# Last block of a routed expert kernel: early products and W2 splits written out in program order, and the next expert's rows asked for ahead of its weights

## The chip, the cores and the metric

The kernel runs on one core of one Trainium2 chip. The metric is device time in microseconds (us) of one launch. TensorE does the matrix products, VectorE and ScalarE the elementwise work and the evictions from PSUM, GpSimd (POOL) some elementwise work and the indirect DMAs, SyncE (SP) issues the other DMAs.

## What is computed

Three parts run one after the other. A linear attention with decay (2 batches, 8 heads, 768 positions, head size 64, blocks of 64 positions) gives x of 1536 tokens by 512. A gated layer follows, and then a layer of eight experts of which each token uses two:

```
x = sigmoid(x @ w_gate) * (x @ w_val) @ w_out            # 512 -> 1536 -> 512

noisy = x @ w_gate2 + log1p(exp(x @ w_noise)) * noise    # 8 logits a token
top2  = two largest of noisy;  top2_w = softmax over the two
for e in range(8):
    h = max(x[tokens of e] @ w1[e], 0)                   # 512 -> 1024
    out[tokens of e] += top2_w * (h @ w2[e])             # 1024 -> 512
```

Inputs and output are float32. Products are made exact enough by splitting each operand into a rounded high part and the low remainder, and adding three products (high x high, high x low, low x high).

## The kernel before

The tokens are handled as 12 tiles of 128. The change lies where the second part ends and the experts begin.

**Products of the second part.** For each tile t, 36 products (`L417`: 12 blocks fb of 128 hidden features, three products each) add up in the PSUM tile `px[t]`. Their left operand `gs` is made by `parts(t, f4)` for four blocks at a time: ScalarE copies (`L68`), VectorE subtracts (`L69`). `product(half)` does two blocks; `products(*steps)` does six halves and calls the given steps between them.

**Route of a tile.** `route(t)` is a generator; each `seg(t)` runs it to its next `yield`: the row copy out of `px` (`L422` ScalarE, `L423` VectorE); four transposes by TensorE and their copy `x2t` (`L428`, `L431`, `L432`); the logits' products and their copy `lq` (`L436`, `L438`); the second logits product, the softplus, the two largest and their masks (`L441` to `L466`, small VectorE and ScalarE instructions of 128x8); the rank of each token in its expert by two products (`L469`, `L470`), weights, slot numbers `ix`, and two indirect scatters of the row by GpSimd into the experts' lists `xg_d` in memory (`L481`). The generators of successive tiles overlap: tile t-2 ends and tile t-1 runs while tile t's products are done. The PSUM tile `ps` of the route has one buffer.

**Expert 0's early part.** The lists are built so that expert 0's first `EARLY` = 256 rows are complete three tiles before the end. They are loaded early (`early_in`: `xg0`, `tg0`). `columns` turns 128 rows into the transposed operand `XT`: VectorE transposes (`L343`), ScalarE copies the high part (`L345`), VectorE subtracts (`L346`). `hidden` then does, for each of eight blocks f of hidden features, 12 products (`L355`) into `pm` (four PSUM buffers), ScalarE's eviction with relu (`L357`) and VectorE's low part (`L358`). `early_hidden` calls it for the 256 rows and puts one half of a W2 split behind each block: ScalarE copies (`L68`), and here GpSimd subtracts (`L69` with `nc.gpsimd`).

**What sets the order.** Up to and with this block, the instructions of TensorE, VectorE, ScalarE and GpSimd are ordered by the planner of the framework, which may move an instruction ahead of others written before it; SP's queue has the order as written. From expert 0's remaining part on, TensorE, ScalarE and VectorE are in the order as written too (`manual_schedule`), each engine strictly one instruction after the other.

**After the block.** `rows_in` and `tags_in` ask for expert 0's rows 256 to 432 once the last scatters are in memory. Output rows of its first 256 rows follow (`L367`, 48 products), under which the remaining rows are turned into columns; then the remaining rows' products (`L355`, 128x176), within which the splits of expert 1's w1 and its columns (`cols(1, ...)`) are put; then the output rows of blocks 2 and 3. SP's queue there reads `ei`, the expert's number, and asks for expert 1: `w1_in(1)` is two loads of 1 MB into `wraw` (three buffers); `fetch(1)` is four loads of rows into `xg` and four of tags into `tg`, each with one buffer that must be free of expert 0's data.

Of the kernel before, what the change touches and what calls it, by code (L numbers as in the profile page):

```python
# [9 lines left out]
F32 = mybir.dt.float32  # L10
# [4 lines left out]
AF = mybir.ActivationFunctionType  # L15
OP = mybir.AluOpType
# [4 lines left out]
DM = 512  # L21
DB = DM // 128
NCH = NT // 128
CPB = 6
FF = 1536
FB = FF // 128
E = 8
F2 = 1024
FB2 = F2 // 128
# [4 lines left out]
EARLY = 256  # L34
# [9 lines left out]
def tile_fused(ctx, tc, qkv, lam, wgv, wout, wgn, noise, w1, w2, out):  # L44
    nc = tc.nc
# [61 lines left out]
    with tc.tile_pool(name="att", bufs=2, reuse_waits="tile") as att, \  # L107
# [24 lines left out]
        n = 1  # L132
# [114 lines left out]
    for a in range(4):  # L247
        p = slice(32 * a, 32 * a + 32)
# [12 lines left out]
    for i in range(4):  # L261
        n = (NT + NDUMP) // 4
# [12 lines left out]
    pxp = tc.alloc_tile_pool(name="pxp", bufs=2, space=PSUM, reuse_waits="tile")  # L275
    with tc.tile_pool(name="p1p", bufs=3, space=PSUM, reuse_waits="tile") as p1p:
        src = [wgv[i] for i in range(FB)] + [wout[i] for i in range(FB // 2)]
        wo = []
        for fb in range(len(src)):
# [28 lines left out]
    mpsum = tc.alloc_tile_pool(name="mpsum", bufs=4, space=PSUM, reuse_waits="tile")  # L308
# [23 lines left out]
    def tags_in(tg, blocks, first):  # L332

        c, m, b = blocks[0]
        k = len(blocks)
        return nc.sync.dma_start(tg[:m, b:b + k],
                                 rows_of(first + c, m * k)(DM, 1 + E).rearrange("(k p) w -> p k w", p=m))

    def columns(t, xg, xT, lo, hi):

        c, n = slice(lo, hi), hi - lo
        t = t[:, :DB * n].rearrange("p (d n) -> p d n", d=DB)
        nc.vector.transpose(out=t.rearrange("p d (s t) -> p s d t", t=32),  # L343
                            in_=xg[:, lo // 32:hi // 32].rearrange("p s (d b) -> p s d b", b=32))
        nc.scalar.activation(xT[:, 0, :, c], t, AF.Copy)  # L345
        nc.vector.tensor_tensor(xT[:, 1, :, c], t, xT[:, 0, :, c], op=OP.subtract)  # L346

    def hidden(W1, xT, hT, lo, hi, fs=range(FB2), pp=None):
        for f in fs:
            w = W1[f // 2][:, :, :, (f % 2) * 128:(f % 2 + 1) * 128]  # L350
            p = (pp or mpsum).tile([128, 512], F32, name="pm")[:, :hi - lo]
            i = 0
            for d in range(DB):
                for a, b in ((0, 0), (0, 1), (1, 0)):
                    nc.tensor.matmul(p, w[:, a, d], xT[:, b, d, lo:hi], start=(i == 0), stop=(i == 3 * DB - 1))  # L355
                    i += 1
# [25 lines left out]
    W1, W2 = {}, {}  # L382
    raw1, raw2 = [expert_raw(w1, 0, j) for j in range(2)], [expert_raw(w2, 0, j) for j in range(2)]
    scat = []
    with tc.tile_pool(name="p2", bufs=2, side="right", reuse_waits="tile") as p2, \
            tc.tile_pool(name="p2p", bufs=2, space=PSUM, reuse_waits="tile") as p2p:
        rows, px, gs, last = {}, {}, {}, []
# [32 lines left out]
        def route(t):  # L420
# [23 lines left out]
            na, u, y, l, c, ns, mx, em, m1, m2, dl, sc = [sm[:, i] for i in range(12)]  # L444
            mm = p2.tile([128, E], BF, name="mm")

            nc.scalar.activation(na, zz, AF.Abs)
            nc.scalar.activation(u, na, AF.Exp, scale=-1.0)
            nc.vector.tensor_scalar(y, u, 1.0, None, op0=OP.add)
            nc.scalar.activation(l, y, AF.Ln)  # L450
            nc.vector.scalar_tensor_tensor(c, y, -1.0, u, op0=OP.add, op1=OP.subtract)
# [4 lines left out]
            nc.vector.tensor_tensor(l, l, noi[:, t], op=OP.mult)  # L456
            nc.vector.tensor_tensor(ns, l, lg, op=OP.add)
            nc.vector.max(mx, ns)
            mi = p2.tile([128, E], U32, name="mi")
            nc.vector.max_index(mi, mx, ns)  # L460
            nc.vector.tensor_copy(sc[:, 0:2], mi[:, 0:2])
# [10 lines left out]
            nc.vector.tensor_scalar(sc[:, 3:4], sc[:, 2:3], 1e-9, None, op0=OP.add)  # L472
            nc.vector.reciprocal(sc[:, 3:4], sc[:, 3:4])
            nc.vector.tensor_scalar(row[:, DM + 1:], em, sc[:, 3:4], None, op0=OP.mult)
            ix = p2.tile([128, 2], I32, name="ix")
            for k, m in enumerate((m1, m2)):
                nc.vector.scalar_tensor_tensor(c, pr, 1.0, m, op0=OP.mult, op1=OP.mult,
# [33 lines left out]
        def seg(t):  # L511
            return lambda: next(R[t], None)
# [10 lines left out]
        def early_in():  # L523
            scat.extend(rows_in(xg0, 0, EARLY, 0) + [tags_in(tg0, B0[:2], 0)])

        products([], [wo5(0)], [], [wo5(1)], [], [], [], [seg(0)], [seg(0)], [seg(0)], [seg(0)], [seg(1)])
        for t in range(2, NCH):
            steps = [[seg(t - 2), seg(t - 1)], [seg(t - 1)], [seg(t - 1)], [], [], [seg(t)]]
            if t > 2 and w1_todo:
                steps[3].append(lambda: after(w1_todo.pop(0)))  # L530
            if t == NCH - LATE + 1:
                big = arena.tile([128, 12288], F32R, name="big", tag="a48")
                XT = [big[:, :8 * MAXC].rearrange("p (x d n) -> p x d n", x=2, d=DB), None]
                hT = big[:, 8 * MAXC:24 * MAXC].rearrange("p (x f n) -> p x f n", x=2, f=FB2)
                xg0 = xgp.tile([128, MAXC // 32, 128], F32, name="xg")
                tg0 = xgp.tile([128, MAXC // 32, 1 + E], F32, name="tg", bufs=1)
                steps[1].append(early_in)
            if t == NCH - 1:
                for i in range(2):
                    steps[i].append(lambda i=i: columns(p2.tile([128, DB * 128], F32, name="xf", bufs=1), xg0, XT[0], i * EARLY // 2, (i + 1) * EARLY // 2))  # L540
            products(*steps)
        W1[0] = [w1view(w) for w in W1[0]]
        w = [wtile() for i in range(4)]
        W2[0] = [w2view(x) for x in w]
        w2_todo = [h for i in range(4) for h in halves(raw2[i // 2][:, (i % 2) * 1024:(i % 2 + 1) * 1024], w[i], nc.gpsimd)]

        def early_hidden(*fs):
            for f in fs:
                hidden(W1[0], XT[0], hT, 0, EARLY, [f])
                w2_todo.pop(0)()  # L550

        t = NCH - 1
        seg(t - 1)()
        early_hidden(0)
        seg(t)()
        early_hidden(1)
        seg(t)()
        early_hidden(2)
        seg(t)()
        early_hidden(3, 4, 5)  # L560
        seg(t)()
        pc = p2p.tile([128, E], F32, name="ps", bufs=1)
        nc.tensor.matmul(pc, ones, macc, start=True, stop=True)
        rows_in(xg0, EARLY, MAXC, 0)
        tags_in(tg0, B0[2:], 0)

        tab = consts.tile([128, 4, E], F32, name="tab")
        cnt, key, srt, er = [tab[:, i] for i in range(4)]
# [18 lines left out]
    with tc.manual_schedule(engines={mybir.EngineType.PE, mybir.EngineType.Activation, mybir.EngineType.DVE}), \  # L587
# [53 lines left out]
        def fetch(i):  # L641

            n, bl = plan[i]
            if i not in regs:
                regs[i] = nc.values_load(ei[0:1, i - 1:i], engines=eng, min_val=0, max_val=E - 1)
            e = regs[i]
            XG[i] = xgp.tile([128, MAXC // 32, 128], F32, name="xg")
            tg[i] = xgp.tile([128, MAXC // 32, 1 + E], F32, name="tg", bufs=1)
            m = (n + 31) // 32
            rows_in(XG[i], 0, 32 * m, e * NT)  # L650
            if natural(i):
                for b in same(bl):
# [250 lines left out]
```

## Time and profile before

| what | value |
|---|---|
| median of 3 runs | 695.37 us (693.76 to 696.55) |
| profiled execution | 694.17 us, span 692.0 us |
| TensorE (PE) busy, of the span | 661.3 us, 96% |
| VectorE (DVE) busy | 466.9 us, 67% |
| ScalarE (ACT) busy | 241.7 us, 35% |
| GpSimd (POOL) busy | 196.6 us, 28% |
| mean granted clock of TensorE | 0.981 of full speed |

Busy time is from the first to the last cycle of each instruction; PEld is TensorE's weight load, which overlaps the products. The profiled execution lies 1.2 us below the median of the runs. The span is from the first to the last instruction; the rest is ahead of it and behind. In the page's row of 40 slices of 17.3 us, TensorE is at nine tenths or more nearly throughout after the first slices, save for the slices around 370 and 430 us.

### The profile page before, as it was taken

What the parts mean: (1) busy time and instruction counts of PE and PEld (TensorE: products, weight loads), DVE (VectorE), ACT (ScalarE), POOL (GpSimd) and SP (SyncE); (2) the same over time, 40 slices, a digit from 0 to 9 for tenths busy, and PEclk for the clock granted to TensorE, in tenths of its full rate; (3) what the DMA queues carried; (4) which work ended last, traced back from release to release, by engine and by line L of the source; (5) the groups of instructions that cost most, each with busy time, mean ns of one, the idle gap of its engine ahead of it and who ended that gap; (6) DMA issues with size and microseconds to landing.
All of it is one profiled execution on the core that took longest, in us unless ns stands there. A gap on an engine that the chain in (4) does not pass through costs nothing. (4 is left out here: it accounts for less than half of the span.)

```text
span 692.0 us, 10373 instructions
## 1 busy us (share of the span) xinstructions
PE 661.3 (96%) x3792; PEld 571.1 (83%) x3793; DVE 466.9 (67%) x1158; ACT 241.7 (35%) x482; POOL 196.6 (28%) x191
## 2 busy tenths in 40 slices
PE   7989999999999999999995998999999999999993
PEld 4877888888888887777773996999999999999982
DVE  3679539999955637777778647565767676767610
ACT  1123223334322223434344214353444444444410
POOL 5541000000000002221227220103838483848401
PEclk9999999999999999999998899999999999999998
DMA  8899943333331101113111187735777676676512
GB/s 254 297 398 378 320 176 123 122 122 121 123 122 61 62 0 62 64 48 107 63 68 56 42 232 196 208 94 153 153 190 156 160 182 183 147 201 156 59 13 35
DMA packets 55417, 98.74 MB, mean 143 GB/s; under 512 B 13938, under 2 KB 37498, under 8 KB 48962
## 3 DMA queue, kind: packets, MB, share of 16 engines
q1 hardware_dynamic: 42290, 84.71, 36.7%
q0 software_dynamic: 13072, 13.32, 11.6%
q8 instruction: 31, 0.51, 0.3%
q14 instruction: 24, 0.20, 0.1%
HBM read 73.11 MB, written 24.91 MB: 142 GB/s over the span
## 5 line engine op out<-in xcount | busy, mean ns | idle before, releaser
L296 PE MATMUL pg<-xh,wspl 128*128 128x512 f32 x576 | 177.5, 389 | 0.0
L675 POOL DMA_INDIRECT out<-y,sids x67 | 109.5, 1635 | 97.0 <-DVE y L689 78.1
L296 PEld LDWEIGHTS pg<-xh,wspl 128*128 128x128 f32 x576 | 108.1, 188 | 22.5 <-issue 0.2
L296 PE MATMUL pg<-xl,wspl 128*128 128x512 f32 x288 | 112.0, 389 | 0.0
L417 PE MATMUL px<-wspl,gs 128*128 128x512 f32 x432 | 108.2, 399 | 0.7 <-DVE gs L69 0.4
L417 PEld LDWEIGHTS px<-wspl,gs 128*128 128x128 f32 x432 | 78.4, 188 | 18.6 <-issue 2.2
L378 PE MATMUL pm<-big,wspl 128*128 128x440 f32 (+4 forms) x480 | 90.8, 349 | 0.7 <-DVE big L358 0.7
L378 PEld LDWEIGHTS pm<-big,wspl 128*128 128x128 f32 x480 | 87.9, 188 | 2.9 <-DVE big L358 1.1
L355 PE MATMUL pm<-big,w1s 128*128 128x256 f32 (+4 forms) x480 | 78.9, 324 | 8.1 <-ACT big L345 8.1
L355 PEld LDWEIGHTS pm<-big,w1s 128*128 128x128 f32 x480 | 76.5, 194 | 9.7 <-ACT big L345 8.6
L355 PE MATMUL pm<-xt,w1s 128*128 128x440 f32 (+3 forms) x384 | 71.3, 346 | 0.0
L355 PEld LDWEIGHTS pm<-xt,w1s 128*128 128x128 f32 x384 | 69.5, 188 | 1.4
L424 POOL COPY row<-tid 128x1 int32<-128x1 int32 x12 | 3.8, 317 | 225.9 <-PE pg L296 203.3
L357 ACT ACTIVATE big<-pm 128x256 fp32r<-128x256 f32 (+8 forms) x72 | 34.0, 472 | 92.7 <-PE pm L355 92.0
L296 PEld LDWEIGHTS pg<-xl,wspl 128*128 128x128 f32 x288 | 54.1, 188 | 11.3
L358 DVE SCALAR_TENSOR_TENSOR big<-pm,big 128x256 fp32r<-128x256 f32 (+8 forms) x72 | 38.0, 528 | 35.2 <-ACT big L357 34.9
L367 PE MATMUL px<-wspl,big 128*128 128x512 f32 (+2 forms) x240 | 57.9, 400 | 1.9 <-ACT big L357 1.6
L367 PEld LDWEIGHTS px<-wspl,big 128*128 128x128 f32 (+2 forms) x240 | 43.8, 184 | 14.9 <-ACT big L357 2.5
L300 DVE TENSOR_TENSOR g<-g,pg 128x512 f32<-128x512 f32 x36 | 24.6, 683 | 46.4 <-PE pg L296 46.3
L299 ACT ACTIVATE g<-pg 128x512 f32<-128x512 f32 x36 | 21.4, 595 | 75.1 <-PE pg L296 75.0
L481 POOL DMA_INDIRECT xg_d<-row,ix x24 | 24.9, 1038 | 69.7 <-ACT x2t L432 28.8
L69 DVE TENSOR_TENSOR w1s<-wraw,w1s 128x512 fp32r<-128x512 f32 x64 | 42.5, 682 | 0.5 <-ACT w1s L68 0.4
(159 smaller groups left out, 811.7 us busy)
## 6 DMA issues: line engine op xcount, KB each, us to landing
wraw<-w SPq DMA_DIRECT2D x32, 1024.0 KB, 5.2
qkv<-qkv SPq DMA_DIRECT2D x24, 512.0 KB, 7.1
wraw<-wgv SPq DMA_DIRECT2D x12, 1024.0 KB, 11.5
xg_d<-z SPq DMA_DIRECT2D x8, 911.8 KB, 16.9
wraw<-wout SPq DMA_DIRECT2D x6, 1024.0 KB, 4.8
out<-z SPq DMA_DIRECT2D x4, 1024.0 KB, 12.9
xg<-xg_d SPq DMA_DIRECT2D x12, 208.0 KB, 3.4
xg<-xg_d SPq DMA_DIRECT2D x8, 224.0 KB, 6.2
```

The source lines that it names most:

```text
L69: eng.tensor_tensor(dst[:, 1], raw, dst[:, 0], op=OP.subtract))
L296: nc.tensor.matmul(p, w[:, a, v, d], x[:, d, sl], start=(i == 0), stop=(i == 3 * DB - 1))
L299: nc.scalar.activation(G[t][:, fb], pp[0], AF.Sigmoid)
L300: nc.vector.tensor_tensor(G[t][:, fb], G[t][:, fb], pp[1], op=OP.mult)
L355: nc.tensor.matmul(p, w[:, a, d], xT[:, b, d, lo:hi], start=(i == 0), stop=(i == 3 * DB - 1))
L357: a = nc.scalar.activation(hT[:, 0, f, lo:hi], p, AF.Relu)
L358: v = nc.vector.scalar_tensor_tensor(hT[:, 1, f, lo:hi], p, 0.0, hT[:, 0, f, lo:hi], op0=OP.max, op1=OP.subtract)
L367: nc.tensor.matmul(p, hT[:, a, f, c:c + m], W2[f // 2][:, x, f % 2], start=(i == 0), stop=(i == 3 * FB2 - 1))
L378: nc.tensor.matmul(p, w[:, a], hT[:, b, f, lo:hi], start=(i == 0), stop=(i == 3 * FB2 - 1))
L417: nc.tensor.matmul(px[t], g[:, a, f], w[:, b], start=(fb == 0 and i == 0), stop=(fb == FB - 1 and i == 2))
L481: s = nc.gpsimd.indirect_dma_start(out=xg_d, out_offset=IndirectOffsetOnAxis(ap=ix[:, k:k + 1], axis=0), in_=row, in_offset=None)
L675: s = nc.gpsimd.indirect_dma_start(out=dst, out_offset=IndirectOffsetOnAxis(ap=ids, axis=0), in_=y, in_offset=None, compute_op=OP.add)
```

## The change

Four edits. (1) The W2 splits' subtraction moves from GpSimd to VectorE. (2) The products of the last tile (t = 11), the rests of the routes of tiles 9 to 11, expert 0's first two column steps, its early products and the W2 splits are put into one block in which TensorE, ScalarE and VectorE follow the order as written; the early products become a generator of single products, of which `fill(n)` does n. (3) `route` gets three more `yield`s, and `seg(t, n)` runs n pieces, so that the loop of the earlier tiles does the same pieces as before. (4) `fetch(1)` goes ahead of `w1_in(1)`.

```diff
             nc.scalar.activation(u, na, AF.Exp, scale=-1.0)
+            yield
             nc.vector.tensor_scalar(y, u, 1.0, None, op0=OP.add)
...
             nc.vector.max(mx, ns)
+            yield
             mi = p2.tile([128, E], U32, name="mi")
...
             nc.vector.tensor_scalar(row[:, DM + 1:], em, sc[:, 3:4], None, op0=OP.mult)
+            yield
             ix = p2.tile([128, 2], I32, name="ix")
...
-        for t in range(2, NCH):
-            steps = [[seg(t - 2), seg(t - 1)], [seg(t - 1)], [seg(t - 1)], [], [], [seg(t)]]
+        for t in range(2, NCH - 1):
+            steps = [[seg(t - 2, 2), seg(t - 1)], [seg(t - 1)], [seg(t - 1, 3)], [], [], [seg(t)]]
...
-            if t == NCH - 1:
-                for i in range(2):
-                    steps[i].append(lambda i=i: columns(p2.tile([128, DB * 128], F32, name="xf", bufs=1), xg0, XT[0], i * EARLY // 2, (i + 1) * EARLY // 2))
...
-        w2_todo = [h for i in range(4) for h in halves(raw2[i // 2][...], w[i], nc.gpsimd)]
-        def early_hidden(*fs):
-            for f in fs:
-                hidden(W1[0], XT[0], hT, 0, EARLY, [f])
+        w2_todo = [h for i in range(4) for h in halves(raw2[i // 2][...], w[i])]
+        last_block = tc.manual_schedule(engines={PE, Activation, DVE})
+        last_block.__enter__()
+        def early_col(i):
+            yield nc.vector.transpose(...)          # from xg0 into xf
+            yield nc.scalar.activation(XT[0][:, 0, :, c], xf, AF.Copy)
+            yield nc.vector.tensor_tensor(XT[0][:, 1, :, c], xf, XT[0][:, 0, :, c], op=OP.subtract)
+        def fbs(*fs): ...                           # three products of px[t] for each block
+        def early_mms(): ...                        # generator of the 96 early products
+        def end_act(n=1): ...                       # relu eviction on ScalarE
+        def end_dve(n=1): ...                       # low part on VectorE
+        def fill(n): ...                            # n early products
+        def split_w2(n=1): ...                      # n halves of W2
-        seg(t - 1)()
-        early_hidden(0)
-        seg(t)()
-        early_hidden(1)
-        seg(t)()
-        early_hidden(2)
-        seg(t)()
-        early_hidden(3, 4, 5)
-        seg(t)()
+        parts(t, 1); fbs(0); seg(t - 2, 2)(); seg(t - 1)(); next(C[0])
+        fbs(1, 2); seg(t - 1)(); fbs(3); next(C[0]); parts(t, 2); fbs(4)
+        seg(t - 1)(); next(C[0]); fbs(5, 6, 7, 8, 9, 10, 11)
+        seg(t - 1)(); next(C[1]); seg(t - 1)(); next(C[1]); next(C[1]); seg(t)()
+        fill(6); seg(t - 1)(); seg(t)(); seg(t - 1)(); split_w2()
+        fill(6); seg(t)(); split_w2(); fill(11); end_act(); seg(t)(); end_dve()
+        fill(1); end_act(); end_dve(); seg(t)(); fill(12); end_act(); seg(t)()
+        fill(16); end_act(); seg(t, 2)(); fill(8); end_act()
         pc = p2p.tile([128, E], F32, name="ps", bufs=1)
         nc.tensor.matmul(pc, ones, macc, start=True, stop=True)
         rows_in(xg0, EARLY, MAXC, 0)
         tags_in(tg0, B0[2:], 0)
+        end_dve(2); split_w2(2); fill(12); end_act(); end_dve(2); split_w2()
+        fill(12); end_act(); end_dve(); split_w2(); fill(12); end_act(); end_dve(); split_w2(2)
...
-        early_hidden(6, 7)
+        last_block.__exit__(None, None, None)
...
         regs[1] = nc.values_load(ei[0:1, 0:1], engines=eng, min_val=0, max_val=E - 1)
+        fetch(1)
         w1_in(1)
-        fetch(1)
         give(0, 1, 128, output_rows(pxp, W2[0], hT, 128, 128))
```

(Statements that the diff has on lines of their own are joined by semicolons here.)

## Rows read from the trace of the kernel before

**Rows 1.** Busy time by stretch: PE, PEld, DVE, ACT, POOL, granted clock, DMA share, GB/s
```profile
372.60:380.80 8.20, 0.06 (x1) 0.00 (x0) 7.96 (x7) 0.89 (x3) 6.24 (x8) 0.68 0.00 0
380.80:385.60 4.80, 4.79 (x22) 4.64 (x23) 2.82 (x18) 0.82 (x3) 0.00 (x0) 0.50 0.01 3
...
426.80:430.20 3.40, 3.40 (x9) 2.11 (x8) 2.82 (x6) 3.30 (x7) 0.00 (x0) 0.50 1.06 331
434.00:464.00 30.00, 30.00 (x152) 28.18 (x151) 17.56 (x29) 12.67 (x25) 1.74 (x1) 1.00 0.47 152
```

**Rows 2.** Waits of PE, 360 to 440 us: total, times, longest
```profile
PE pm L355 <- ACT big L345: 8.1, 1, 8.1
```

**Rows 3.** Timeline around 370 us: start, length, engine, line, operation
```profile
370.00 4.97 POOL L69 TENSOR_TENSOR wspl<-wraw,wspl 128x512 fp32r<-128x512 f32 x4
...
370.14 9.21 DVE L346 TENSOR_TENSOR big<-xf,big 128x512 fp32r<-128x512 f32 x1 [1.69 <-ACT big L345]
...
379.38 0.71 DVE L343 STREAM_TRANSPOSE xf<-xg 128x512 f32<-128x512 f32 x1
```

**Rows 4.** Timeline of earlier tiles' routes, 345 to 363 us
```profile
345.67 0.43 DVE L431 COPY x2t<-pt 128x256 f32<-128x256 f32 x1
...
346.95 0.43 PE L436 MATMUL ps<-x2t,wgn_s 128*32 128x128 f32 x8
...
358.73 5.71 PE L417 MATMUL px<-wspl,gs 128*128 128x512 f32 x24
...
359.37 0.17 DVE L449 TENSOR_SCALAR sm<-sm 128x8 f32<-128x8 f32 x1 [0.50 <-ACT sm L448]
...
361.24 0.67 DVE L69 TENSOR_TENSOR gs<-g,gs 128x512 fp32r<-128x512 f32 x1
...
362.56 0.23 DVE L463 SCALAR_TENSOR_TENSOR mm<-io,sm 128x8 bf16<-128x8 f32 x1
```

**Rows 5.** Timeline: early products, output rows, and a split on VectorE
```profile
348.39 0.68 DVE L69 TENSOR_TENSOR w1s<-wraw,w1s 128x512 fp32r<-128x512 f32 x1
...
389.48 4.44 PE L355 MATMUL pm<-big,w1s 128*128 128x256 f32 x35
...
396.95 11.07 PE L367 MATMUL px<-wspl,big 128*128 128x512 f32 x48
```

**Rows 6.** Timeline of SP's DMA issues, 355 to 470 us
```profile
400.29 1.76 SPq L329 DMA_DIRECT2D xg<-xg_d  x4
...
403.66 1.00 SPq L61 DMA_DIRECT2D wraw<-w  x2
406.50 2.05 SPq L329 DMA_DIRECT2D xg<-xg_d  x4
408.81 6.38 SPq L656 DMA_DIRECT2D tg<-xg_d  x4
...
463.65 1.92 SPq L329 DMA_DIRECT2D xg<-xg_d  x4
...
467.89 1.50 SPq L61 DMA_DIRECT2D wraw<-w  x2
```

**Rows 7.** DMA issues, 467.7 to 468.3 us: count, KB each, us to landing
```profile
wraw<-w SPq DMA_DIRECT2D x1, 1024.0 KB, 5.2
```

**Rows 8.** Timeline of the last scatter, columns, w1 split and last eviction
```profile
397.30 0.98 POOL L481 DMA_INDIRECT xg_d<-row,ix  x1 [0.30 <-issue]
...
404.13 0.58 DVE L343 STREAM_TRANSPOSE xf<-xg 128x384 f32<-128x384 f32 x1 [5.78 <-DMA xg<-xg_d]
...
407.06 0.56 DVE L346 TENSOR_TENSOR big<-xf,big 128x384 fp32r<-128x384 f32 x1 [0.59 <-ACT big L345]
...
413.60 0.62 ACT L68 ACTIVATE w1s<-wraw 128x512 fp32r<-128x512 f32 x1
...
418.44 0.71 DVE L343 STREAM_TRANSPOSE xf<-xg 128x512 f32<-128x512 f32 x1 [2.15 <-DMA xg<-xg_d]
...
425.44 0.30 ACT L357 ACTIVATE big<-pm 128x176 fp32r<-128x176 f32 x1
```

More of the change, by code (lines that the diff above doesn't have):

```diff
@@ L509, in products, with seg, f @@
                     f()
-        def seg(t):
-            return lambda: next(R[t], None)
+        def seg(t, n=1):
+            def f():
+                for _ in range(n):
+                    next(R[t], None)
+            return f
         def wo5(i):
@@ L524, in early_in @@
             scat.extend(rows_in(xg0, 0, EARLY, 0) + [tags_in(tg0, B0[:2], 0)])
-        products([], [wo5(0)], [], [wo5(1)], [], [], [], [seg(0)], [seg(0)], [seg(0)], [seg(0)], [seg(1)])
-        for t in range(2, NCH):
-            steps = [[seg(t - 2), seg(t - 1)], [seg(t - 1)], [seg(t - 1)], [], [], [seg(t)]]
+        products([], [wo5(0)], [], [wo5(1)], [], [], [], [seg(0)], [seg(0)], [seg(0)], [seg(0, 3)], [seg(1)])
+        for t in range(2, NCH - 1):
+            steps = [[seg(t - 2, 2), seg(t - 1)], [seg(t - 1)], [seg(t - 1, 3)], [], [], [seg(t)]]
             if t > 2 and w1_todo:
@@ L544, in tile_fused @@
         W2[0] = [w2view(x) for x in w]
-        w2_todo = [h for i in range(4) for h in halves(raw2[i // 2][:, (i % 2) * 1024:(i % 2 + 1) * 1024], w[i], nc.gpsimd)]
-        def early_hidden(*fs):
-            for f in fs:
-                hidden(W1[0], XT[0], hT, 0, EARLY, [f])
-                w2_todo.pop(0)()
-        t = NCH - 1
-        seg(t - 1)()
-        early_hidden(0)
+        w2_todo = [h for i in range(4) for h in halves(raw2[i // 2][:, (i % 2) * 1024:(i % 2 + 1) * 1024], w[i])]
+        last_block = tc.manual_schedule(engines={mybir.EngineType.PE, mybir.EngineType.Activation,
+                                                 mybir.EngineType.DVE})
@@ new lines, in tile_fused @@
+        last_block.__enter__()
+        t = NCH - 1
+        def early_col(i):
+            lo, n = i * EARLY // 2, EARLY // 2
+            xf = p2.tile([128, DB * 128], F32, name="xf", bufs=1)[:, :DB * n].rearrange("p (d n) -> p d n", d=DB)
+            c = slice(lo, lo + n)
+            yield nc.vector.transpose(out=xf.rearrange("p d (s t) -> p s d t", t=32),
+                                      in_=xg0[:, lo // 32:(lo + n) // 32].rearrange("p s (d b) -> p s d b", b=32))
+            yield nc.scalar.activation(XT[0][:, 0, :, c], xf, AF.Copy)
+            yield nc.vector.tensor_tensor(XT[0][:, 1, :, c], xf, XT[0][:, 0, :, c], op=OP.subtract)
@@ new lines, in fbs, with early_mms @@
+        def fbs(*fs):
+            for fb in fs:
+                for i, (a, b) in enumerate(((0, 0), (0, 1), (1, 0))):
+                    nc.tensor.matmul(px[t], gs[t, fb // 4][:, a, fb % 4], wo[fb // 2][:, b, fb % 2],
+                                     start=(fb == 0 and i == 0), stop=(fb == FB - 1 and i == 2))
+        def early_mms():
+            for f in range(FB2):
+                p = mpsum.tile([128, 512], F32, name="pm")[:, :EARLY]
+                i = 0
+                for d in range(DB):
+                    for a, b in ((0, 0), (0, 1), (1, 0)):
+                        nc.tensor.matmul(p, W1[0][f // 2][:, a, d, f % 2 * 128:(f % 2 + 1) * 128],
+                                         XT[0][:, b, d, :EARLY], start=(i == 0), stop=(i == 3 * DB - 1))
+                        i += 1
+                        if i == 3 * DB:
+                            ends.append((hT[:, 0, f, :EARLY], hT[:, 1, f, :EARLY], p))
+                        yield
@@ new lines, in end_act, with end_dve, fill, split_w2 @@
+        def end_act(n=1):
+            for _ in range(n):
+                h, l, p = ends.pop(0)
+                nc.scalar.activation(h, p, AF.Relu)
+                subs.append((l, p, h))
+        def end_dve(n=1):
+            for _ in range(n):
+                l, p, h = subs.pop(0)
+                nc.vector.scalar_tensor_tensor(l, p, 0.0, h, op0=OP.max, op1=OP.subtract)
+        def fill(n):
+            for _ in range(n):
+                next(E0)
+        def split_w2(n=1):
+            for _ in range(n):
+                w2_todo.pop(0)()
@@ new lines, in tile_fused @@
+        ends, subs, E0, C = [], [], early_mms(), [early_col(i) for i in range(2)]
+        px[t] = pxp.tile([128, DM], F32, name="px")
+        parts(t, 1)
+        fbs(0)
+        seg(t - 2, 2)()
+        seg(t - 1)()
+        next(C[0])
+        fbs(1, 2)
+        seg(t - 1)()
+        fbs(3)
+        next(C[0])
+        parts(t, 2)
+        fbs(4)
+        seg(t - 1)()
+        next(C[0])
+        fbs(5, 6, 7, 8, 9, 10, 11)
+        seg(t - 1)()
+        next(C[1])
+        seg(t - 1)()
+        next(C[1])
@@ L555, in tile_fused @@
+        next(C[1])
         seg(t)()
-        early_hidden(1)
+        fill(6)
+        seg(t - 1)()
         seg(t)()
-        early_hidden(2)
+        seg(t - 1)()
+        split_w2()
+        fill(6)
         seg(t)()
-        early_hidden(3, 4, 5)
+        split_w2()
+        fill(11)
+        end_act()
         seg(t)()
+        end_dve()
+        fill(1)
+        end_act()
+        end_dve()
+        seg(t)()
+        fill(12)
+        end_act()
+        seg(t)()
+        fill(16)
+        end_act()
@@ L562, in tile_fused @@
+        seg(t, 2)()
+        fill(8)
+        end_act()
         pc = p2p.tile([128, E], F32, name="ps", bufs=1)
@@ L565, in tile_fused @@
         tags_in(tg0, B0[2:], 0)
+        end_dve(2)
+        split_w2(2)
+        fill(12)
+        end_act()
+        end_dve(2)
+        split_w2()
+        fill(12)
+        end_act()
+        end_dve()
+        split_w2()
+        fill(12)
+        end_act()
+        end_dve()
+        split_w2(2)
         tab = consts.tile([128, 4, E], F32, name="tab")
```

## The prediction

> **What bounds the kernel now.** I read the table of stretches first, for TensorE. From 434 us on, in the first of the later experts, it is busy throughout at a granted clock of 1.00 [rows 1]: such a stretch shrinks only if TensorE does less, and the change takes nothing from it. What can be won lies before, where three rows are not full. In 372.6 to 380.8 us TensorE does nothing; in 380.8 to 385.6 us it is busy but the granted clock is 0.50, the lower of its two levels (1.2 GHz against 2.4); in 426.8 to 430.2 us it is 0.50 again [rows 1]. The list of waits names who ended the first: one wait of 8.1 us of L355 (expert 0's early products) on ScalarE's L345, the copy of the column tile [rows 2]. The timeline then shows what stood behind the first: VectorE's L346, a subtraction of a 128x512 tile, ran from 370.14 to 379.35, 9.21 us, while GpSimd made the W2 splits (L69) from 370.00 on [rows 3]. The same form takes 0.68 us elsewhere [rows 5]. The second column tile's transpose could start only behind it, at 379.38 [rows 3], ScalarE's copy behind that, and the products behind the copy.
>
> So the old order has two losses. Around the last block: 8.15 us idle and 4.8 us at half clock, which is 2.4 us of lost work: 10.5 us. Around expert 0's remaining products (TensorE enters them at 396.95 + 11.07 = 408.0 us [rows 5] and the next expert at 434.0 [rows 1]): the work is 96 products, some 10.9 us, and 48 of L367 at 11.07/48 = 0.231, 11.1 us [rows 5]. 26.0 - 22.0 = 4.0 us lost, of which 3.4 x 0.5 = 1.7 us are the half clock [rows 1].
>
> **The W2 splits on VectorE.** Eight halves leave GpSimd and cost VectorE 0.68 us each [rows 5], 5.4 us, interleaved with the early products. These last 96 x 0.127 = 12.2 us [rows 5], in which VectorE otherwise has the last routes and eight evictions, so they find room. What they remove is the cause of the 9.21 us subtraction, and with it the 8.15 us wait and the half clock that followed it: up to 10.5 us. The trace shows the stretched instruction lasting as long as GpSimd's run of eight splits, not one [rows 3]. The Trainium skill, "SBUF — State Buffer", section "Who interferes with whom", says that a VectorE instruction with two SBUF inputs and a GpSimd instruction that reads SBUF exclude each other, and that the loser waits for the other's whole instruction. By that rule the wait would be one split, 4.97/4 = 1.24 us by [rows 3], and 7 of the 8.15 us would have another cause that stays; the row has the larger price, and the rule's smaller one is a rival below.
>
> **The order by program.** The rest is what TensorE waits for in the new order. It starts tile 11 at 363.0 in both kernels (18 of the 24 products in [rows 4], of 0.238 each, are tile 10's). From there to L367 the old kernel takes 33.95 us; without 8.15 and 2.4 this is 23.4 us of work. To this I add the new waits, following each queue in the order of the diff:
> - Tile 10's transposes behind only three products: 0.5 us, since its row copies run one after the other.
> - Tile 10's logits. VectorE must first do the gs subtraction (0.67, ended at 364.9), then eight small instructions of tile 9's ranks, which the new order writes ahead of tile 10's copy (0.16 each). The copy x2t starts near 366.1, and TensorE's logits start 1.28 behind it, with ScalarE's half between, as from 345.67 to 346.95 [rows 4]: 367.3. It was done with fbs(1, 2) at 366.5: 0.85 us.
> - The first early product. VectorE's queue before it: gs subtraction 0.67 from 369.1 on, first column subtraction 0.68, route up to the mask of choices 2.8 (359.37 to 362.79, less 0.6 for the gs subtraction inside it [rows 4]), second transpose 0.71 [rows 3] and subtraction 0.68: about 374.6, on TensorE 375.0. Its products end at 374.4: 0.6 us. This is the place of the old 8.15.
> - Tile 11's logits, behind its row copies, four transposes and x2t with two fills of six products as cover: 0.6 us.
> - Tile 11's ranks: logits at 380.0, two ScalarE instructions and a queued eviction until 380.9, 2.8 us on VectorE and some for the overlap with evictions, 0.4 to hand over: 384.35, against fills that end at 383.5: 0.9 us.
> - The rest (transposes of tile 11, counts): 0.45 us.
>
> Together 3.9 us. L367 then starts at 363.0 + 23.4 + 3.9 = 390.3 instead of 396.95: **6.6 us** earlier. From both sides: if VectorE and ScalarE keep up everywhere, 10.5; if each of the five larger waits is twice as long, 3.2. I take 6.6, since the pieces are measured one by one.
>
> What is late next? The second half of W2 is split by 392.5 and L367 needs its last pieces only from 394.3, so this is covered. Tile 11's slots are known at 385.2, its two scatters end at 388.3, the remaining rows are asked for 2.0 us later, as before (398.28 to 400.29 [rows 6, 8]), at 390.3, and are usable 3.84 us after that (404.13 less 400.29), at 394.2. VectorE is past the splits and the table at 394.8; the two column steps of 3.5 us (404.13 to 407.62 [rows 8]) end at 398.2, while L367 covers until 390.3 + 11.07 = 401.4. Slack 3.2 us; without it the products would wait for the difference.
>
> **The second expert's rows ahead of its weights.** SP's queue gets eight issues in front of two of 1 MB. In the old order the weights went at 403.66, the rows at 406.50 (they wait until the buffer's old rows are transposed) and the tags at 408.81 [rows 6]; the rows came so late that VectorE waited 2.15 us until 418.44, and the last eviction of that stage stood behind it at 425.44 [rows 8]. Without that wait this eviction comes at 423.3 and its low part on VectorE near 424.5, while TensorE, after 10.9 us of products and 21 of L367 (4.85 us), wants it at 423.7: 0.8 us of wait are left, and most of the idle that led to the half clock at 426.8 is gone. Gain: 2.15 and up to 1.7, 3.8 us.
>
> The price is the weights. They are issued behind rows that still wait for the buffer. In new time it is free at 397.0, when the second column step has transposed. For the interval from there I use the next expert whose three requests stand in this order: 463.65 rows, 467.89 weights, landed 5.2 us later [rows 6, 7]: 9.4 us, so 406.4; the tags' own wait (until 399.3) adds 0.2. The first split of them was at 413.60 [rows 8], 5.6 us after the stage began, now 401.4 + 5.6 = 407.0. So the weights arrive just in time by this row, and late if the scatter-adds of the first output rows share the engines. Lower bound of lateness 0; upper bound: the tags take 6.38 us to issue as at 408.81, instead of the 2.3 us between the end of the rows' issue at 465.57 and 467.89 [rows 6], which is 4.1 us late. All evictions behind that split wait as well, on both engines, and for them the output rows. I take 0.9, nearer to the row with the same order, and half of the clock's 1.7: 0.8 + 0.9 + 0.85 = 2.55 us lost; by the same terms the old order loses 0.8 + 2.15 + 1.7 = 4.65, of which 4.0 show in the whole. Gain **2.0 us**, between 4.0 - 2.55 and 4.65 - 2.55; bounds -2.0 (0.8 + 4.1 + 1.7 = 6.6 lost) and +3.8.
>
> Behind it TensorE is full to the end [rows 1], and all moves up together. The route's three extra yields change nothing: the calls in the loop count them.
>
> **Sum.** 6.6 + 2.0 = 8.6 us. The profiled execution is 694.17 us (span 692.0), so it would become 685.6; the median of the runs is 1.2 us above it, so **686.8 us**.
>
> **Rivals.**
> 1. *Weights starve.* The first part holds, but rows and tags fill the queue so that w1 is 3 to 4 us late: TensorE waits 4.5 us where it waited 2.9, and the clock falls as before. Gain 6.6 - 2 = 4.6, 690.8. For it: the tags' 6.38 us; against: the issue at 467.89, right behind rows and tags. Chance 0.12.
> 2. *More waits than counted.* In program order one late instruction holds its whole queue; with doubled waits the gain is 3.2 + 2.0, 690.2. Chance 0.08.
> 3. *The wait stays.* If the cause of the 9.21 us were mostly something other than the splits, only one split's 1.24 us and the second part's 2.0 go: 692.1. Against it: it began with the splits and ended when they did. The rule of the Trainium skill quoted above comes to this time. Chance 0.04.
> 4. *Slower: the clock.* The early products now come in fills of 6 to 16 with waits of 0.5 to 0.9 us between. If the lower level is granted throughout them, 96 x 0.127 = 12.2 us are added, and 8.6 becomes -3.6: 699.0. It decides from 8.6 / 12.2 = 70% of the early products on. For it: both idle stretches were followed by 0.50 [rows 1]; against: those were 8 us without work, and a stage broken by several waits in a row, while here the longest wait that I count is 0.9 us. The Trainium skill, "TensorE: Matmul & The Clock Gate", section "A second HAM failure mode: psum-queue depth-cycling", reports such swinging with frequent short idles between groups of matmuls; no row here shows it for waits this short. Chance 0.04.
>
> **How the numbers follow.** The forecast has 0.72; its own range is 683 to 690.5. What a measurement of this kernel can tell from no change is about 0.5%, 3.5 us: below 691.9 is faster, above 698.8 slower. The forecast lies wholly below, rivals 1 and 2 for about three quarters (0.15 of 0.20), rival 3 half; rival 4 splits between same and slower. This gives faster 0.88 at face value; I shift a little for what in-order queues may do that the pieces don't show: 0.86, 0.10, 0.04. The range that leaves out 2 in 10: low 682.5 (both parts near their best, 8.5 + 3.8, and some), high 691.8 (rivals 1 and 2).
>
> **What would show it.** Right: no VectorE subtraction above 1 us in the last block; TensorE's longest wait there under 1.5 us and the granted clock near 1.00; L367 begins at about 390; the second expert's first transpose waits for no DMA, and the first w1 split waits less than 2 us. Wrong: L367 later than 393, a granted clock of 0.5 for more than 3 us in the early products, or TensorE entering the second expert later than 26 us after expert 0's remaining products began.

## The result and the profile after

| | before | after |
|---|---|---|
| median (4 runs each, timed in turn) | 695.23 us (693.76 to 696.55) | 688.97 us (688.70 to 690.16) |
| ratio, 95% interval | 1 | 0.9917 (0.9898 to 0.9935) |
| span of the profiled execution | 692.0 us | 687.2 us |
| mean granted clock of TensorE | 0.981 | 0.986 |

The change gains 5.8 us (0.83% of 695.23), 4.5 to 7.1 by the interval. Forecast were 8.6 us and 686.8; the measured median lies 2.2 us above that, inside the range and inside the forecast's own range. So the direction was right. By its two terms the sum was not: the first gave more than forecast, and the second, forecast as a gain, became a loss. That the total came out so near is in part luck, since the two errors have opposite signs.

The spans differ by less than the runs, 4.8 us, because of something outside the change. The attention part, which is the same code in both, ends later in the profile after: the first product of the gated layer starts 2.2 us later, and tile 10's row copy is later by the same 2.2. I therefore count from that row copy. The timeline of the kernel before (start, length, engine, line, operation):

```profile
61.55 0.50 PE L296 MATMUL pg<-xh,wspl 128*128 128x512 f32 x1
...
363.17 0.39 ACT L422 ACTIVATE row<-px 128x256 f32<-128x256 f32 x1 [0.74 <-PE px L417]
...
407.86 10.85 PE L355 MATMUL pm<-big,w1s 128*128 128x176 f32 x96
...
433.95 19.36 PE L355 MATMUL pm<-xt,w1s 128*128 128x440 f32 x96
```

The timeline of the kernel after, from the same product on through the last block and expert 0's remaining part:

```profile
63.75 0.50 PE L296 MATMUL pg<-xh,wspl 128*128 128x512 f32 x1
...
365.35 0.39 ACT L422 ACTIVATE row<-px 128x256 f32<-128x256 f32 x1 [0.73 <-PE px L417]
...
376.70 0.69 DVE L565 TENSOR_TENSOR big<-xf,big 128x512 fp32r<-128x512 f32 x1 [0.72 <-ACT big L564]
...
387.00 0.86 PE L367 MATMUL px<-wspl,big 128*128 128x512 f32 x3
...
392.16 10.16 PE L367 MATMUL px<-wspl,big 128*128 128x512 f32 x44
...
399.45 1.98 SPq L329 DMA_DIRECT2D xg<-xg_d  x4
401.68 2.05 SPq L760 DMA_DIRECT2D tg<-xg_d  x4
402.16 10.85 PE L355 MATMUL pm<-big,w1s 128*128 128x176 f32 x96
403.98 16.42 SPq L61 DMA_DIRECT2D wraw<-w  x4
412.12 0.63 ACT L68 ACTIVATE w1s<-wraw 128x512 fp32r<-128x512 f32 x1 [4.11 <-DMA wraw<-w]
414.24 0.70 DVE L343 STREAM_TRANSPOSE xf<-xg 128x512 f32<-128x512 f32 x1
421.58 8.02 PE L367 MATMUL px<-wspl,big 128*88 128x512 f32 x27 [1.63 <-ACT big L357]
429.44 2.77 PE L355 MATMUL pm<-xt,w1s 128*128 128x440 f32 x13
```

Two stretches hold all of it. **A** runs from tile 10's row copy to expert 0's remaining products (`L355`, 128x176): 363.17 to 407.86 before, 44.7 us; 365.35 to 402.16 after, 36.8. **B** runs from there to the second expert's products (128x440): 407.86 to 433.95 before, 26.1 us (the prediction, which took the end of the group ahead as the start of B, has 26.0); 402.16 to 429.44 after, 27.3. A gives 7.9 back, B takes 1.2: 6.7 us, within the measured 4.5 to 7.1.

Busy time of the kernel after by stretch (length, then PE, PEld, DVE, ACT, POOL, granted clock, DMA share, GB/s):

```profile
372.60:380.80 8.20, 7.14 (x47) 5.54 (x46) 5.99 (x31) 2.61 (x8) 0.62 (x4) 1.00 0.01 2
380.80:392.00 11.20, 11.02 (x89) 10.44 (x88) 9.35 (x41) 5.21 (x15) 4.31 (x4) 1.00 0.23 87
421.60:425.40 3.80, 3.80 (x10) 2.33 (x11) 3.23 (x7) 2.71 (x6) 0.00 (x0) 0.55 0.97 336
434.00:464.00 30.00, 30.00 (x152) 28.17 (x151) 19.00 (x37) 15.26 (x29) 0.00 (x0) 1.00 0.50 152
```

Waits of PE in the kernel after, 340 to 440 us (total, times, longest):

```profile
PE px L367 <- ACT big L357: 3.3, 2, 1.6
PE pm L580 <- ACT big L564: 0.6, 1, 0.6
PE ps L436 <- DVE x2t L431: 0.6, 1, 0.6
PE pm L580 <- DVE big L565: 0.3, 1, 0.3
PE ps L472 <- DVE mm L465: 0.2, 1, 0.2
```

These lines show that the 8.1 us wait [rows 2] and the idle and half-clock stretches around 376 us [rows 1] are gone, with TensorE busy 7.14 of 8.20 and 11.02 of 11.20 at a granted clock of 1.00. The subtraction that lasted 9.21 us [rows 3] lasts 0.69 (`L565`). In B, TensorE waits twice for ScalarE's eviction (3.3 us in all; the second wait, 1.63, is followed by a granted clock of 0.55 for 3.8 us), and those evictions stand behind a w1 split that waited 4.11 us for its weights, which landed 8.1 us after their issue at 403.98. Full stretches such as 434 to 464 are as they were.

### The profile page after: what moved, and what is told of

Same layout as the page of the kernel before. It is cut to its first block, busy times and chain, and to the rows that moved or that the text cites. A ratio compares the mean times of both kernels' runs of the same rounds, so it can differ in the third digit from the quotient of the medians.

```text
span 687.2 us, 10367 instructions
## 1 busy us (share of the span) xinstructions
PE 659.2 (96%) x3792; PEld 569.4 (83%) x3793; DVE 465.4 (68%) x1166; ACT 241.5 (35%) x482; POOL 187.3 (27%) x183
## 3 DMA queue, kind: packets, MB, share of 16 engines
q0 software_dynamic: 13072, 13.32, 11.7%
## 5 line engine op out<-in xcount | busy, mean ns | idle before, releaser
L417 PE MATMUL px<-wspl,gs 128*128 128x512 f32 x396 | 99.2, 399 | 0.7 <-DVE gs L69 0.4
L417 PEld LDWEIGHTS px<-wspl,gs 128*128 128x128 f32 x396 | 71.8, 188 | 17.2 <-issue 2.0
L355 PE MATMUL pm<-xt,w1s 128*128 128x440 f32 (+3 forms) x384 | 71.3, 346 | 0.0
L355 PEld LDWEIGHTS pm<-xt,w1s 128*128 128x128 f32 x384 | 69.5, 188 | 1.3
L355 PE MATMUL pm<-big,w1s 128*128 128x176 f32 (+3 forms) x384 | 63.2, 324 | 0.0
L355 PEld LDWEIGHTS pm<-big,w1s 128*128 128x128 f32 x384 | 62.8, 189 | 0.1
L367 PE MATMUL px<-wspl,big 128*128 128x512 f32 (+2 forms) x240 | 58.1, 400 | 3.3 <-ACT big L357 3.3
L357 ACT ACTIVATE big<-pm 128x176 fp32r<-128x176 f32 (+7 forms) x64 | 30.9, 483 | 83.1 <-PE pm L355 83.1
L358 DVE SCALAR_TENSOR_TENSOR big<-pm,big 128x176 fp32r<-128x176 f32 (+7 forms) x64 | 34.7, 542 | 33.3 <-ACT big L357 33.3
L367 PEld LDWEIGHTS px<-wspl,big 128*128 128x128 f32 (+2 forms) x240 | 43.7, 184 | 16.0 <-ACT big L357 3.9
```

What stands on the lines that cost most here:

```text
L367: nc.tensor.matmul(p, hT[:, a, f, c:c + m], W2[f // 2][:, x, f % 2], start=(i == 0), stop=(i == 3 * FB2 - 1))
L417: nc.tensor.matmul(px[t], g[:, a, f], w[:, b], start=(fb == 0 and i == 0), stop=(fb == FB - 1 and i == 2))
```

## Experiments

Three factors were taken apart: the engine of the W2 splits (GpSimd G or VectorE V), the order in the last block (the planner's or the program's), and the order of the requests for expert 1 (weights first, rows first, or half the weights, rows, then the other half). A and B are in us from each profile; A + B less 70.8 can be held against the timed ratio. A profile shows one execution and the time is a median of several, so the last column and the timed difference lie up to 2 us apart: e3's profiled execution is the slowest of its six (685.57 us), e5's the fastest (685.88), and their A and B carry that.

| kernel | splits | order | requests | median us | ratio (95% interval) | A | B | A + B - 70.8 |
|---|---|---|---|---|---|---|---|---|
| before | G | planner | weights | 695.23 | 1 | 44.7 | 26.1 | 0 |
| e2 | G | planner | rows | 697.62 | 1.0049 (1.0031 to 1.0067) | 44.5 | 29.5 | +3.2 |
| e5 | G | program | weights | 690.42 | 0.9946 (0.9926 to 0.9967) | 41.3 | 24.4 | -5.1 |
| after | V | program | rows | 688.97 | 0.9917 (0.9898 to 0.9935) | 36.8 | 27.3 | -6.7 |
| e3 | V | planner | weights | 683.32 | 0.9836 (0.9810 to 0.9861) | 34.2 | 27.1 | -9.5 |
| e1 | V | program | weights | 683.34 | 0.9839 (0.9814 to 0.9864) | 36.8 | 23.5 | -10.5 |
| e4 | V | program | half | 682.62 | 0.9826 (0.9802 to 0.9851) | 36.8 | 22.3 | -11.7 |
| e8 | V | planner | half | 680.88 | 0.9799 (0.9783 to 0.9814) | 34.2 | 22.7 | -13.9 |

**e1: weights first again, in the changed kernel.**

```diff
-        fetch(1)
         w1_in(1)
+        fetch(1)
```

> The changed kernel with the second expert's two weight loads ahead of its rows again, as before the change; all else as changed. Theory (the rows in front starve the weights): the stretch from expert 0's remaining products to the second expert, 27.3 us in the changed kernel and 26.0 before, falls to 23 to 25 us; the first w1 split waits for no DMA (4.1 us in the changed kernel); the time is 2 to 4 us below the changed kernel, about 686. Rival (the weights are late because of the scatter-adds and the tags, wherever they stand): the split still waits 2 us or more, and the time is within 1 us of the changed kernel's 689. Rival of the forecast (rows first is worth 2 us): the time rises to about 691.

Measured: 683.34 us, ratio 0.9839, so the order rows first costs the changed kernel 0.78%, 5.4 us, more than the 2 to 4 expected. B, 23.5 instead of 27.3, accounts for 3.8 of them; where the rest lies the profiles don't show. Its timeline:

```profile
394.92 1.00 SPq L61 DMA_DIRECT2D wraw<-w  x2
...
397.68 2.16 SPq L329 DMA_DIRECT2D xg<-xg_d  x4
...
400.40 10.85 PE L355 MATMUL pm<-big,w1s 128*128 128x176 f32 x96
...
409.95 0.71 DVE L343 STREAM_TRANSPOSE xf<-xg 128x512 f32<-128x512 f32 x1 [1.13 <-DMA xg<-xg_d]
...
423.87 18.36 PE L355 MATMUL pm<-xt,w1s 128*128 128x440 f32 x91
```

The row copy is at 363.60 here. Measured from it, the weights go out 31.3 us later, in the changed kernel 38.6 (403.98 - 365.35). The rows go out 34.1 us later in both (397.68 - 363.60, 399.45 - 365.35). Standing first didn't get the rows issued any sooner: they wait for their buffer, and the weights, which had nothing to wait for, waited behind them.

It did make the rows land sooner. The four row loads, from issue to landing, first in the kernel before (weights ahead of them), then in the changed kernel (rows ahead):

```profile
DMA to landing us min/median/max: 6.2/7.4/10.1
```

```profile
DMA to landing us min/median/max: 3.0/4.0/4.7
```

Behind 2 MB of weights the last rows land some 5 us later, and with the weights first (e1) the second expert's first transpose waits 1.13 us for them, where in the changed kernel it waits for none. Each order has its price; here that of rows first is the larger.

**e2: rows first alone, in the kernel before.**

```diff
-        w1_in(1)
         fetch(1)
+        w1_in(1)
```

> The kernel before with this one edit: the second expert's rows and tags asked for ahead of its weights. Theory: the weights now stand behind rows that wait until 406.5 us, so the first w1 split waits 3 to 6 us for them, and the stretch from expert 0's remaining products to the second expert grows from 26.0 us to 27 to 28.5; the time is 1 to 2.5 us above before. Forecast as it stood: the stretch falls to 24 us, the time by 2.

Measured: 697.62, slower by 0.49% (0.31 to 0.67), 3.4 us, more than the 1 to 2.5 expected; B, 29.5, is past the expected 28.5 too. The timeline and ScalarE's wait of this kernel:

```profile
405.38 1.98 SPq L329 DMA_DIRECT2D xg<-xg_d  x4
...
410.54 16.17 SPq L61 DMA_DIRECT2D wraw<-w  x4
```

```profile
ACT w1s L68 <- DMA wraw<-w: 6.0, 1, 6.0
```

Counted from the row copy (362.09 here, 363.17 before) the weights leave SP 48.5 us later, 8.0 us more than the 40.5 of the kernel before (403.66 [rows 6]), and ScalarE waits 6.0 us for them. So this part of the change loses in both kernels.

**e3: splits alone, in the kernel before.**

```diff
-  w2_todo = [h for i in range(4) for h in halves(..., w[i], nc.gpsimd)]
+  w2_todo = [h for i in range(4) for h in halves(..., w[i])]
```

> The kernel before with this one edit: the W2 splits' subtraction on VectorE, the planner keeping the order. Theory (GpSimd's splits held VectorE's subtraction): no 128x512 subtraction of VectorE above 1 us; the 8.1 us wait of the early products falls to 3 to 5 us, since the planner had put the splits' copies ahead of the columns and their eight subtractions (5 us) now stand in VectorE's queue there; time 3 to 6 us below before. Rival (another cause, as a lock for only one instruction would need): the long subtraction and at least 6 us of the wait stay, time within 2 us of before.

Measured: 683.32 us, ratio 0.9836, a gain of 11.4 us where 3 to 6 were expected, twice that of the whole change. My expectation of a wait that stays in part was wrong: the timeline and the waits of this kernel show none in the block that is longer than 0.2 us.

```profile
PE pm L355 <- ACT big L345: 0.2, 1, 0.2
```

```profile
363.76 0.39 ACT L422 ACTIVATE row<-px 128x256 f32<-128x256 f32 x1 [0.76 <-PE px L417]
...
387.08 11.07 PE L367 MATMUL px<-wspl,big 128*128 128x512 f32 x48
...
409.55 0.71 DVE L343 STREAM_TRANSPOSE xf<-xg 128x512 f32<-128x512 f32 x1 [2.81 <-DMA xg<-xg_d]
```

With VectorE free of GpSimd, A is 34.2 us in the planner's order and 36.8 in the program's. The written order is not needed for the gain; it costs 2.6 us of A. In this kernel the shorter A runs into late rows: 2.81 us of wait, and the granted clock falls to 0.61 from 416.9 to 421.0, which makes B 27.1 in the execution profiled. With the weights first the two orders take the same time (683.32 and 683.34).

**e5: the written order alone** (the changed kernel with its splits back on GpSimd and the weights first).

```diff
-  w2_todo = [h for i in range(4) for h in halves(..., w[i])]
+  w2_todo = [h for i in range(4) for h in halves(..., w[i], nc.gpsimd)]
-        fetch(1)
         w1_in(1)
+        fetch(1)
```

> The kernel before with this one edit: the last block in program order, the W2 splits still on GpSimd and the weights ahead of the rows. Theory (the splits on GpSimd are the whole loss, the order is worth nothing in itself): program order already puts both column steps ahead of the splits, so the 8.1 us wait goes even so; but the splits now meet the routes' small instructions and VectorE shows single instructions stretched to 1.3 us or more; the time is 2 to 6 us above the same kernel with the splits on VectorE (683.3), 685 to 689. Rival (the order is what matters, not the engine): within 1 us of 683.3.

Measured: 690.42 us, 0.9946, 7 us slower than the same with the splits on VectorE (e1) and above the 685 to 689 expected. The order alone gains 0.54%, 3.8 us: the wait of 8.1 us is gone. The timeline shows two VectorE instructions held by GpSimd's splits, of small tiles of 128x8 this time; such forms take 0.17 to 0.23 us elsewhere [rows 4]. Behind the first of them TensorE waits 1.7 us, its longest in A.

```profile
378.54 2.54 POOL L69 TENSOR_TENSOR wspl<-wraw,wspl 128x512 fp32r<-128x512 f32 x2
378.60 2.53 DVE L450 TENSOR_SCALAR sm<-sm 128x8 f32<-128x8 f32 x1
...
388.71 7.54 POOL L69 TENSOR_TENSOR wspl<-wraw,wspl 128x512 fp32r<-128x512 f32 x6
...
392.83 3.46 DVE L674 SCALAR_TENSOR_TENSOR tab<-tab,io 128x8 f32<-128x8 f32 x1
```

**e9: half of the splits on GpSimd**, in the kernel before, to see whether VectorE is held for one GpSimd instruction or for a run of them.

```diff
-  w2_todo = [h for i in range(4) for h in halves(..., w[i], nc.gpsimd)]
+  w2_todo = [h for i in range(4) for h in halves(..., w[i], nc.gpsimd if i >= 2 else nc.vector)]
```

> The kernel before with the first four of the eight W2 split halves on VectorE and the last four left on GpSimd. Theory (VectorE's subtraction is held for as long as GpSimd's splits follow each other): a 128x512 subtraction of VectorE of 3 to 5.5 us, or two shorter ones, a wait of the early products of 2 to 4 us, time 3 to 6 us above the kernel with all on VectorE (683.3). Rival (held for one instruction at most): no subtraction above 2 us, wait under 1 us, time within 1.5 us of 683.3.

Measured: 688.11 us (686.94 to 689.85), ratio 0.9904 (0.9886 to 0.9922), 4.8 us slower than all splits on VectorE; A is 39.7, B 24.9. The timeline, and the stretch behind the wait:

```profile
373.10 2.49 POOL L69 TENSOR_TENSOR wspl<-wraw,wspl 128x512 fp32r<-128x512 f32 x2
373.45 0.94 DVE L453 TENSOR_TENSOR sm<-sm 128x8 f32<-128x8 f32 x1
...
374.58 1.56 DVE L346 TENSOR_TENSOR big<-xf,big 128x512 fp32r<-128x512 f32 x1
...
376.19 1.22 PE L355 MATMUL pm<-big,w1s 128*128 128x256 f32 x4 [2.21 <-DVE big L346]
```

```profile
376.20:382.50 6.30, 6.30 (x29) 6.14 (x30) 3.28 (x25) 0.59 (x2) 0.67 (x1) 0.50 0.00 0
```

The price came as expected, its form did not. No VectorE instruction lasts longer than 1.56 us: between two GpSimd splits a small one got in, so each was held for about one split. But the holds added up to a wait of 2.21 us, and the 6.3 us at the lower clock behind it cost half their length, 3.15 us, more. Together they are 5.4 of the 5.5 us by which A is longer than in e3.

**e4: half the weights ahead of the rows**, in the changed kernel.

```diff
+        raw[1] = [expert_raw(w1, regs[1], 0)]
         fetch(1)
-        w1_in(1)
+        raw[1].append(expert_raw(w1, regs[1], 1))
```

> The changed kernel with the first of the two 1 MB loads of w1 ahead of the rows and the second behind the tags. Theory: SP can issue the first load some 3 us before the rows' buffer is free, when the DMA engines idle, so it delays neither; first split and first transpose of the second expert wait for no DMA; the stretch is 23 to 24.5 us (0.8 us of wait from VectorE's queue and some half clock left) and the time 3 to 4 us below the changed kernel, 685 to 686, and 0 to 1 us below the order with both weights first. Rival (the second load's lateness comes to matter): a wait of a later w1 split, stretch over 25 us.

Measured: 682.62 us, 0.9826, B 22.3 us against the 22.0 of work that the prediction summed: TensorE runs through it without one wait for an eviction, and neither the first w1 split nor the first transpose of the second expert waits for a DMA. That is better than expected (685 to 686, B of 23 to 24.5). The interval overlaps that of weights first (e1), so by time the two can't be told apart.

**e10: the scatter-adds of expert 0's first two blocks left out**, in the changed kernel, to see how much of the weights' lateness is theirs.

```diff
-                add(i, out, ids, y[:m])
+                if i or b > 1:
+                    add(i, out, ids, y[:m])
```

> The changed kernel with the two scatter-adds of expert 0's first two blocks of output rows left out (those 256 tokens lose expert 0's part). Theory (GpSimd's scatter-adds take about 2.9 us of the DMA engines' time while the first load of w1 is in flight, 404 to 412 us): the first load lands 5 to 5.5 us after its issue instead of 8.1; the first w1 split waits 0.5 to 1.5 us instead of 4.1; the stretch from expert 0's remaining products to the second expert falls from 27.3 to 23 to 25 us, the time by 2 to 4 us, to 685 to 687. Rival (the two 1 MB loads of w1 share the engines and land together, whatever else runs): the first lands 7.5 us or more after its issue and the stretch stays at 26.5 us or more.

First the DMA queues of the changed kernel, 404 to 406 us (packets, MB, and the time that the packets took, as a share of the 16 engines' time; the two shares add up to more than 100%, so packets overlap), and its first weights (count, KB, us to landing):

```profile
q1 hardware_dynamic: 1522, 0.13, 80.1%
q0 software_dynamic: 98, 0.20, 55.9%
```

```profile
wraw<-w SPq DMA_DIRECT2D x1, 1024.0 KB, 8.1
```

Then the kernel without the adds: ScalarE's wait and the timeline.

```profile
ACT w1s L68 <- DMA wraw<-w: 2.3, 1, 2.3
```

```profile
400.39 10.85 PE L355 MATMUL pm<-big,w1s 128*128 128x176 f32 x96
...
408.54 0.63 ACT L68 ACTIVATE w1s<-wraw 128x512 fp32r<-128x512 f32 x1 [2.30 <-DMA wraw<-w]
...
426.18 16.16 PE L355 MATMUL pm<-xt,w1s 128*128 128x440 f32 x80
```

Measured: 685.68 us (683.86 to 687.20), ratio 0.9861 (0.9829 to 0.9892). The weights, issued at 402.51, are used 6.0 us later instead of 8.1; the wait is 2.3 us instead of 4.1, and B 25.8 instead of 27.3. GpSimd's adds are about 2 of the 4.1 us of wait. The other 2.3 us are more than the expectation left (0.5 to 1.5), and B stayed above the 23 to 25 expected; the time is as expected. With the weights first and the adds in place (e1) ScalarE doesn't wait for the weights at all, so the place in the queue makes the adds' 2 us count.

**e8: the two best together**, the kernel before with its planner's order, splits on VectorE, half the weights ahead of the rows. Its edits are those of e3 and e4.

> The kernel before with the splits on VectorE, in the planner's order, and the first 1 MB of w1 ahead of the second expert's rows, the other behind. Theory (the order by program costs 2 to 2.5 us in the last block, and the rows that come late give them back in the kernel with the splits alone): output rows begin some 2 us earlier in the block than in program order, the stretch to the second expert is 22 to 23 us, the time 678 to 680.5, below every kernel so far, 682.6 included. Rival (the remaining rows' chain through memory sets the end, whichever order the block has): the time stays at 682 to 683.5.

Measured: 680.88 us, 0.9799 (0.9783 to 0.9814), the lowest median of all, 2.0% below the kernel before and 8 us below the change, 0.4 us above the range expected and below the rival's. Its interval overlaps e4's (0.9802 to 0.9851), so its lead over e4 isn't clear of noise. The timeline:

```profile
386.64 11.08 PE L367 MATMUL px<-wspl,big 128*128 128x512 f32 x48
...
397.55 11.23 PE L355 MATMUL pm<-big,w1s 128*128 128x176 f32 x96
...
408.62 11.75 PE L367 MATMUL px<-wspl,big 128*88 128x512 f32 x48
...
420.21 19.36 PE L355 MATMUL pm<-xt,w1s 128*128 128x440 f32 x96
```

Each group of products follows the one before without a gap: 11.23, 11.75, then the second expert.

## Why the prediction was right and wrong

**What bounds, and the splits: right.** The splits alone give 11.4 us, and putting half of them back costs 4.8. The 10.5 us read as the loss around the last block [rows 1 to 3] are all won in e3, where A falls by 10.5. The rival of a wait that stays (692.1) fell with e3. The rule of the Trainium skill that is quoted there, one instruction of hold, is what e9 shows, and not what the kernel before shows: 9.21 us there, 2.53 and 3.46 in e5 behind two and about three splits. What decides how many pass before VectorE gets in stays open.

**The order by program: right in kind, 1.3 us too dear.** I added 3.9 us of new waits; A came out 7.9 us shorter instead of 6.6, so they are 2.6, of which the list of waits names 1.7. Tile 10's logits, set at 0.85, waited 0.6; the first early product, set at 0.6, waited 0.6, and a second one 0.3; tile 11's logits, set at 0.6, didn't wait; its ranks, set at 0.9, waited 0.2. And four of `L367`'s products, 0.9 us of work, were done ahead of the others, between the early products, which I had not counted on. What I didn't ask was whether this order is needed: it is these 2.6 us that separate it from the planner's order once VectorE is free (36.8 against 34.2).

**Rows ahead of weights: the step that failed.** "So the weights arrive just in time by this row" put 9.4 us between the rows' turn and the weights' landing, by the next expert [rows 6, 7]. It took 12.65 (399.45 to about 412.1). Of the 3.25 more, 0.3 are the issue (403.98 - 399.45 = 4.53, where [rows 6] has 4.24) and 2.9 the landing (8.1 against 5.2 [rows 7]). The order of the requests was the same in that row; what else the DMA engines had to do was not: in B the packets of GpSimd's scatter-adds of expert 0's first output rows took 55.9% of the engines' time in 404 to 406 us, where the kernel before has no packet of GpSimd's queue from 467.9 to 473.1, and without the two adds the weights are there after 6.0 us (e10). I named this condition in the prediction and gave it no price of its own. What makes the other 0.8 was not tried.

The wait of 4.11 closes with two more of the prediction's numbers. It had the weights 0.6 us ahead of the split (406.4 against 407.0), and the remaining products 4.4 us behind the rows' turn (401.4 - 397.0); they came 2.7 behind it (402.16 - 399.45), 1.7 sooner, because A was shorter than forecast while the columns on VectorE were not as early. The split was wanted 5.85 us into B (408.01) instead of 5.6: -0.6 + 3.25 + 1.7 - 0.25 = 4.1.

The forecast gain of 2.0 became a loss of 1.2 in B against the kernel before, between my bounds; against the same kernel with the weights first it is a loss of 5.4 us in time. That is rival 1 in mechanism, late by the 3 to 4 us that it names (here 4.1). Its time of 690.8 was missed because A gave 1.3 us more and because TensorE's own waits in B were 3.3 us, not its 4.5.

The gain side of that step was read rightly. The rows left SP no sooner, 43.3 us behind the row copy whether the weights stood ahead of them (406.50 - 363.17) or behind them (405.38 - 362.09, e2); but they landed sooner, 4.7 us at most after their issue instead of 10.1, and the wait of 2.15 us [rows 8] went. It was worth less than the weights' lateness, which holds the same evictions. That the two need not be traded the prediction didn't see: with half the weights ahead (e4) neither is waited for.

**The clock: right for the early products, wrong for B.** The slower rival (699.0) did not come: the waits of 0.2 to 0.6 us in the list left the granted clock at 1.00 from 372.6 to 392.0 us. The half clock in B, of which I thought "most" of the cause gone, stayed: 0.55 for 3.8 us behind a wait of 1.63.

**Marks.** Of the marks named, these came: no long subtraction, clock 1.00, no wait above 0.62 us in the block, no DMA wait before the second expert's first transpose. `L367` began 26.8 us after the row copy where 27.1 (390.3 - 363.17) was forecast. These failed: the first w1 split waited 4.11 us instead of less than 2, and B took 27.3 instead of less than 26. The two that failed are both of the second part, which is where the wrong step is.

## What to carry to other kernels

In a queue that works strictly in order, put the request that waits for nothing ahead of the one that waits for a buffer; the latter is issued no later by it, as the rows' turn at 34.1 us in both orders shows. It can land later, as the rows did behind 2 MB (10.1 us instead of 4.7), so ask how much must stand ahead: half of the weights was enough, and B was shortest with it (22.3 and 22.7). An interval taken from a similar place may not hold where other queues are active: look at the shares of all DMA queues in both stretches before the interval becomes a term. And when a change has a cause removed and an order rewritten, try the removal alone first: here it gave twice what both gave together with a reordered queue.

## What the runs showed of the hardware

A VectorE instruction beside a run of GpSimd subtractions was held through eight of them once (9.21 us [rows 3]), through two and about three (2.53 and 3.46 us, for tiles of 128x8), and through one at a time in e9 (0.94 to 1.56 us). Even the mildest form cost 4.8 us: the wait that it led to (2.21 us) was followed by 6.3 us at a granted clock of 0.50. With two of GpSimd's indirect adds left out, a 1 MB load of SP's queue was there 6.0 us after its issue instead of 8.1. And four loads of rows landed up to 10.1 us after their issue behind 2 MB of weights, up to 4.7 ahead of them.
